# Seven quarter products in the last two stages of an attention, GLU and bilinear kernel

## The chip, the cores and the metric

One Trainium2 chip, one of its cores. The metric is the device time of one execution of the whole program in microseconds; a kernel's time is the median of its runs.

## What is computed

The reference is attention with a threshold (four batches, eight heads, 576 positions, head size 64), a gated layer, and a bilinear layer followed by two more matrix products. The change is in the last line of this cut:

```python
x = attn_out.transpose(0, 2, 1, 3).reshape(2304, 512)      # after the attention
g = x @ w_gate                                             # 512 x 1536, float64 on arrival
x = (g * sigmoid(g)) * (x @ w_val) @ w_out                 # 1536 x 512
h = (x @ w1) * (x @ w2)                                    # 512 x 1024 each
out = (h @ w3) @ w_out2                                    # 1024 x 1024, then 1024 x 512
```

[...]

## The kernel before

**Stages.** The program runs through attention; the first unit stage (the GLU, 12 units of 128 of the 1536 columns); the output stage (times `w_out`); the second unit stage (the bilinear product, 8 units of 128 of the 1024 columns); a stage that multiplies `w3` by `w_out2` once, so that the last stage, all 18 tiles of 128 tokens, is a single product with that 1024 x 512 matrix. Below, W is that product of weights, the stage that makes it is the W stage, and the stage after it is the last stage.

**Precision.** Every float32 operand is kept as two parts, a rounded one (`fp32r`) made by a cast on ScalarE and the rest made by a subtraction on VectorE (`rest_of`, L1594 to L1601, whose subtraction is recorded under L1589). A product is three passes (L1547, `mm3`): high by high, high by rest, rest by high. The passes of one accumulating group are matmuls of 128 x 128 weights with 512 or 256 columns.

**Units.** In both unit stages the tokens are four blocks of 512 and one of 256 (`blocks`, L1532). Two pairs of 512-blocks go through `seven` (L1756): their 1024 tokens and the two weight matrices form a 2 x 2 scheme that takes seven products in place of eight (p1 to p7, sums s1 to s4 of the inputs, differences of the weights); L1749 is its matmul, L1768 the copy that ScalarE takes of the running bank between two products, L1776 and L1780 VectorE's sums. The block of 256 goes through `plain` (L1827). Each unit also converts the weights of the next unit (`weights_f`, `weights_2`).

**Conversions to DRAM.** `whole_pair` (L1975) converts 128 x 1024 values of `w_out2` (4 calls) or `w3` (8 calls) and stores them in `v_dram`, from where the W stage loads them (`whole_back`, L2137 to L2141; the load is L2139). Its VectorE lines are L1631, L1634, L1639, L1643 and L1645, its ScalarE lines L426 and L427, its store L1659. Eight of the twelve calls are made in the first unit stage (L2024), three in the output stage (L2108, L2113), the last in the second (L2132).

**The last two stages.** Per group of 128 rows of W, `w3_turn` (L2150) loads a tile of `w3`, turns it with eight transposes (L2157) into two banks, and splits it (L2161, L2163); the group is then 24 matmuls of 512 columns (`go`, L2184), a cast and a subtraction (L2190, L2192). The last stage takes the blocks in the order 0, 1, 3, 4, 2; `h2_all` loads and splits a block (`h_two`: the load is L2034, with 2 KB in a row, the cast L2040), a tile is 24 matmuls of 512 columns, copied to SBUF by VectorE (L2225) or ScalarE (L2228) and stored (L2233).

**What orders the work.** `Program` (L125 to L296) takes steps with an engine, a cost, a due time and what they read and write, and lays all engines' instructions out before the run: an engine takes the step that can start first, by due time within 0.15 us; TensorE never takes one that is due more than 3 us after its oldest open step. Costs are written into the steps (0.6 us for a VectorE subtraction, 1.45 us for 12 matmuls of 256 columns, 4 us until a load has landed). The result is a fixed order for each engine's queue and for SyncE, which issues the transfers: an instruction whose input is late holds everything behind it. 42 tiles (`slot`, 128 x 2 x 512) are shared by all operands of these stages, four PSUM banks T and two double banks S by all products.

## Time and profile before

| | |
|---|---|
| median of three runs | 1071.97 us (1069.6 to 1074.06) |
| profiled execution | 1068.02 us, of which the span is 1066.2 |
| TensorE busy | 1042.2 us, 98% |
| VectorE busy | 838.8 us, 79% |
| ScalarE busy | 644.2 us, 60% |
| GpSimd busy | 286.4 us, 27% |
| DMA queue of SyncE | 161.29 MB, 50.1% of 16 engines |

How to read it: the span is what the engines' records cover; busy times are of that span. Shares over the whole span mix stages with different limits, so the rows further down are of single stages. A matmul's duration includes the way through the array, so the distance between starts says what one costs.

### The profile page before, as it was taken

To read this page: it belongs to the slowest core of one execution; us is meant where nothing else is said; L and a number is where in the kernel's file an instruction comes from. 1 tells how busy PE (TensorE), PEld (TensorE's weight loads), DVE (VectorE), ACT (ScalarE), POOL (GpSimd) and SP (SyncE) were. 2 spreads that over 40 slices of the span, in tenths; PEclk is the share of its full clock that TensorE was granted. 3 is DMA by queue.
4 is the path that set the end of the run, shared out by engine and by line. 5 is a ranking of instruction groups with operands and counts; after the bars stand their busy time and mean duration, and the time that the engine had idled before them with its cause. 6 is when DMAs were issued, how large, how long until landed. Compare 5 with 4: busy or idle time off the path is not lost.

```text
span 1066.2 us, 16931 instructions
## 1 busy us (share of the span) xinstructions
PE 1042.2 (98%) x5834; PEld 908.4 (85%) x5834; DVE 838.8 (79%) x1536; ACT 644.2 (60%) x1368; POOL 286.4 (27%) x307
## 2 busy tenths in 40 slices
PE   7999999999999999999999999999999999999998
PEld 6999999999977888888888889788888887888886
DVE  7999999999996979999999956976867777442320
ACT  6999999999974556656667634644433444242220
POOL 5899999999853000000000000000000000000000
PEclk9999999999999999999999999999999999999999
DMA  7686777766566225454556661551223225621531
GB/s 183 161 213 168 196 189 176 198 164 155 154 187 233 76 82 175 164 199 150 182 164 231 234 217 59 193 183 40 85 89 115 94 104 183 242 80 62 149 117 49
DMA packets 127206, 162.36 MB, mean 152 GB/s; under 512 B 48689, under 2 KB 83313, under 8 KB 127121
## 3 DMA queue, kind: packets, MB, share of 16 engines
q1 hardware_dynamic: 126976, 161.29, 50.1%
q8 instruction: 46, 0.75, 0.3%
q14 instruction: 40, 0.32, 0.1%
q10 hardware_dynamic: 144, 0.00, 0.0%
HBM read 93.47 MB, written 44.19 MB: 129 GB/s over the span
## 4 chain that ended last, share of the span: by engine, by line
PE 73%; DVE 12%; ACT 5%; DMA 4%; issue 2%; POOL 2%; SPq 1%; ACTq 0%; DVEq 0%; POOLq 0%
PE t_bank L1549 25%; PE t_bank L1749 16%; PE s_bank L1749 11%; PE s_bank L1549 6%; PE s_bank L627 5%; PE t_bank L591 4%; PE t_bank L869 3%; DVE slot L1589 2%; DVE P L675 2%; ACT P L684 1%; DVE E L659 1%; DMA x_dram<-xs 1%; POOL AT L376 1%; DMA slot<-v_dram 1%; PE t_bank L881 1%
## 5 line engine op out<-in xcount | busy, mean ns | idle before, releaser
L1549 PE MATMUL t_bank<-slot,slot 128*128 128x512 f32 (+1 forms) x1680 | 339.0, 360 | 1.4 <-DVE slot L1589 1.3
L1549 PEld LDWEIGHTS t_bank<-slot,slot 128*128 128x128 f32 x1680 | 283.9, 189 | 52.1 <-DVE slot L1589 2.4
L1749 PE MATMUL t_bank<-slot,slot 128*128 128x512 f32 x816 | 196.9, 390 | 1.2 <-ACT tmp L1768 1.2
L1589 DVE TENSOR_TENSOR slot<-slot,slot 128x512 fp32r<-128x512 f32 (+1 forms) x247 | 155.5, 664 | 41.7 <-ACT slot L2040 28.9
L1749 PEld LDWEIGHTS t_bank<-slot,slot 128*128 128x128 f32 x816 | 151.9, 188 | 32.8 <-ACT tmp L1768 2.1
L1749 PE MATMUL s_bank<-slot,slot 128*128 128x512 f32 x612 | 147.0, 389 | 0.0
L376 POOL TENSOR_TENSOR AT<-tmp,AT 128x512 fp32r<-128x512 f32 x105 | 137.5, 1309 | 8.8
L1749 PEld LDWEIGHTS s_bank<-slot,slot 128*128 128x128 f32 x612 | 114.9, 188 | 23.9
L1768 ACT COPY tmp<-t_bank 128x512 f32<-128x512 f32 x102 | 59.4, 584 | 114.0 <-PE t_bank L1749 113.9
L675 DVE SCALAR_TENSOR_TENSOR P<-s_bank,stat,E 128x576 f32<-128x576 f32 x144 | 116.4, 812 | 3.1
L684 ACT ACTIVATE P<-P,stat 128x576 f32<-128x576 f32 x144 | 112.6, 782 | 3.4 <-DVE P L675 1.2
L1597 ACT CAST slot<-slot 128x512 fp32r<-128x512 f32 x135 | 81.3, 621 | 53.4 <-DVE slot L1589 20.1
L659 DVE TENSOR_SCALAR_CACHE_REDUCE E<-s_bank,tau_sb 128x576 f32<-128x576 f32 x135 | 108.9, 810 | 4.7 <-PE s_bank L627 3.8
L627 PE MATMUL s_bank<-R,L 128*128 128x288 f32 x512 | 95.4, 308 | 7.9 <-DVE P L675 6.2
L627 PEld LDWEIGHTS s_bank<-R,L 128*128 128x128 f32 x512 | 74.1, 190 | 13.8 <-PE t_bank L591 2.7
L591 PE MATMUL t_bank<-ident,P 128*128 128x128 f32 x640 | 85.3, 273 | 0.4 <-DVE rt L1495 0.4
L1549 PE MATMUL s_bank<-slot,slot 128*128 128x512 f32 (+1 forms) x432 | 84.7, 354 | 0.0
L1549 PEld LDWEIGHTS s_bank<-slot,slot 128*128 128x128 f32 x432 | 71.5, 189 | 11.3
L426 ACT ACTIVATE raw<-raw,ebias 128x512 int32<-128x512 int32 x76 | 58.8, 774 | 29.4 <-DVE slot L1639 28.8
L2040 ACT CAST slot<-slot 128x512 fp32r<-128x512 f32 (+1 forms) x100 | 52.5, 577 | 38.5 <-DMA slot<-h_dram 34.0
L591 PEld LDWEIGHTS t_bank<-ident,P 128*128 128x128 f32 x640 | 73.9, 140 | 1.8 <-DVE rt L1495 0.7
L869 PE MATMUL t_bank<-AT,sp 128*128 128x288 f32 x448 | 74.1, 299 | 0.0
(156 smaller groups left out, 1342.8 us busy)
## 6 DMA issues: line engine op xcount, KB each, us to landing
slot<-h_dram SPq DMA_DIRECT2D x40, 512.0 KB
h_dram<-h SPq DMA_DIRECT2D x34, 512.0 KB
raw<-in_moe_w_dram SPq DMA_DIRECT2D x32, 512.0 KB
raw<-in_moe_w_out_dram SPq DMA_DIRECT2D x20, 512.0 KB
x_dram<-xs SPq DMA_DIRECT2D x64, 144.0 KB
L<-qlo SPq DMA_DIRECT2D x60, 128.0 KB
L<-qhi SPq DMA_DIRECT2D x60, 128.0 KB
raw<-in_moe_w_gate_dram SPq DMA_DIRECT2D x12, 512.0 KB
```

The costliest lines, as they stand in the source:

```text
L376: nc.gpsimd.tensor_tensor(out=lo, in0=src, in1=f32(hi), op=ALU.subtract)
L591: nc.tensor.matmul(bank[:, t * P:(t + 1) * P], lhsT=part, rhs=ident, is_transpose=True, start=(t == 0), stop=(t == len(parts) - 1),)
L627: nc.tensor.matmul(o, lhsT=lhs, rhs=R[:, c:c + HALF], start=(h == hs2[0] and e == 0), stop=(h == hs2[-1] and e == 1),)
L659: nc.vector.tensor_scalar(out=halves(t), in0=sb[:, :, 0:HALF], scalar1=tau_sb, scalar2=None, op0=ALU.add, op1=ALU.min, accum_out=st[:, 0, c],)
L675: nc.vector.scalar_tensor_tensor(out=halves(p_tile(p, i)), in0=sb[:, :, 0:HALF], scalar=st[:, 0, c], in1=halves(t), op0=ALU.is_gt, op1=ALU ...
L684: nc.scalar.activation(out=u, in_=u, func=ACTF.Exp, scale=-FAR, bias=st[:, 1, c], accum_out=sums[p // HP][:, c],)
L869: nc.tensor.matmul(b["t"][:, 0:HALF], lhsT=splits[p, 2][:, 4 * h + c, :, :].rearrange("p a d -> p (a d)"), rhs=AT[h][:, e, c, cs], start=( ...
L1549: nc.tensor.matmul(o, lhsT=lhs(a), rhs=rhs(c), start=(first and i == 0), stop=(last and i == 2))
L1589: nc.vector.tensor_tensor(out=out, in0=x, in1=y, op=ALU.subtract)
L1597: act(lambda: nc.scalar.copy(out=un["t"][:, 0, :], in_=src()), [key], [(un, 0)], 0.52, due, after)
L1749: nc.tensor.matmul(ap(), lhsT=un["t"][:, a, (off + kk) * P:(off + kk + 1) * P], rhs=x[kk]["ap"](c), start=(start and kk == 0 and i == 0), ...
L1768: act(lambda: nc.scalar.copy(out=k[n]["t"], in_=xa()), [(x, 0)], [(k[n], 0)], 0.47, NOW)
```

## The change

`quarters`, `rows_seven` and `stagger` bring a 2 x 2 scheme of seven products to the W stage and the last stage. Two 128-row tiles, each seen as two halves along the 1024 summed values, are the left side, the two halves of rows and of columns of the right matrix the right side; a product is 12 matmuls with 256 columns. The left side's sums s1 to s4 are made per pair of tiles (`quarters`: 11 VectorE operations and 7 casts), the right side's t1 to t4 once (`sums`: 8 subtractions and 8 splits). In `rows_seven` four products run one after the other in the same T bank, with a ScalarE copy after each, and three in two halves of an S bank, each ended by a VectorE addition. `stagger` puts p4 and p3 of one pair behind p1 of the next. W is kept as float32 too (`F["w"]`). The block of 256 tokens keeps the old form (`odd_tile`) and runs first. Loads of the left side in the last stage take 128 columns of all eight rows of `h2_dram` (`tile_in`), 512 bytes in a row. The calls of `whole_pair` in the output stage go to the second unit stage, one in each of the units 2 to 5, and the loads of `w_out2` may start one unit earlier.

The diff, cut to its core:

```diff
@@ rest_of: a list of keys may be given
+        keys = key if isinstance(key, list) else [key]
...
@@ output stage
     panels(0, True, (), 6.0, 1.2)
-    whole_pair(after=at_now(), due=12.0)
     weights_2(0, after=at_now(), due=16.0, step=2.0)
     for j in (2, 3, 4):
-        if j == 3:
-            for i in range(2):
-                whole_pair(after=at_now(), due=8.0 + 12 * i, step=1.6)
         banks = out_banks(j, j != 3)
...
@@ second unit
-        first = at_now()
+        before, first = first, at_now()
         if 1 <= f < NF2 - 1:
             weights_2(f + 1, after=first, due=4.0, step=1.6)
-        if f >= NF2 - 2:
-            whole_pair(after=first, due=4.0)
+        if f > 1:
+            whole_pair(after=first, due=8.0, step=1.6)
...
-    order = (0, 1, 3, 4, 2)
...
-        pe(5.46, go, [q for u in w3s + ps_ for q in both(u)], [(bank, 0)])
...
+    F, U_OF, SUMS = {"p": [], "w": []}, {"p": {}, "w": {}}, {}
     for c in range(NF2 // 2):
-        t = whole_back(c, -14.0 + 2 * c, first)
+        t = whole_back(c, -14.0 + 2 * c, before)
+        F["p"].append((t, both(t)))
+        for e in range(2 if c > 1 else 0):
+            U_OF["p"][2 * c + e] = rest_of(
+                lambda t=t, e=e: t["t"][:, e, :], (t, e), None, -14.0 + 2 * c)
...
+    def tile_in(c, due, after):
+        t = buf("slot", F32)
+        j = max(i for i in range(NB) if blocks[i][0] <= c)
+        sp(lambda: nc.sync.dma_start(
+            out=t["t"].rearrange("p e (f c) -> p (e f) c", c=P),
+            in_=h2_dram[:, :, c:c + P].rearrange("f p c -> p f c"),
+        ), [("h2", f, j) for f in range(NF2)], both(t), 1.2, 5.0, due - 6, after)
+        return t
...
+    def quarters(t, u, due, step=1.3):
+
+        A = {}
+        for key, b, e in (("11", t, 0), ("12", t, 1), ("22", u, 1)):
+            A[key] = half_of(b, e, due)
+            due += step
+        for key, op, o, x, y in (
+            ("s1", ALU.add, (u, 1), (u, 0), (u, 1)), ("s3", ALU.subtract, (u, 0), (t, 0), (u, 0)),
+            ("s2", ALU.subtract, (t, 0), (u, 1), (t, 0)), ("s4", ALU.subtract, (t, 1), (t, 1), (t, 0)),
+        ):
+            ap = lambda k: k[0]["t"][:, k[1], :]
+            dve(lambda o=o, x=x, y=y, op=op: nc.vector.tensor_tensor(
+                out=ap(o), in0=ap(x), in1=ap(y), op=op), [x, y], [o], 0.6, due)
+            A[key] = half_of(*o, due + 0.6)
+            due += step
+        return A
...
+    def sum_of(w, key, h, o, x, y, due):
+        at = lambda k: F[w][h + 2 * k[0]][0]["t"][:, :, k[1] * 256:(k[1] + 1) * 256]
+        on = lambda k: F[w][h + 2 * k[0]][1]
+        dve(lambda: sub(at(o), at(x), at(y)), on(x) + on(y), on(o), 0.6, due)
+        split_of(w, key, h, o, due)
+
+    def sums(w, due):
+        for key, *args in (
+            ("t1", (0, 0), (0, 1), (0, 0)), ("t3", (0, 1), (1, 1), (0, 1)),
+            ("t2", (1, 1), (1, 1), (0, 0)), ("t4", (1, 0), (1, 0), (1, 1)),
+        ):
+            for h in range(2):
+                sum_of(w, key, h, *args, due)
...
+        def product(bank, ap, un, key, start, stop):
+            ws = [right_of(w, key, kk) for kk in range(4)]
+
+            def go():
+                for kk in range(4):
+                    for i, (a, e) in enumerate(PASSES):
+                        nc.tensor.matmul(
+                            ap(), lhsT=un["t"][:, a, kk * P:(kk + 1) * P], rhs=ws[kk][1](e),
+                            start=(start and kk == 0 and i == 0), stop=(kk == 3 and i == 2),
+                            skip_group_check=not start,
+                        )
+
+            return pe(1.45, go, both(un) + [q for u, _ in ws for q in both(u)], [bank])
...
+        def p1():
+            product((x, 0), xa, A["11"], "11", True, False)
+            copy(top, 0)
+
+        def p2():
+            product((yz, 0), y, A["12"], "21", True, True)
+            plus(top, 0, y, (yz, 0))
+
+        def p6():
+            product((x, 0), xa, A["s2"], "t2", False, False)
+            copy(top, 1)
+
+        def p5():
+            product((yz, 1), z, A["s1"], "t1", True, False)
+
+        def p7():
+            product((x, 0), xa, A["s3"], "t3", False, False)
+            copy(low, 1)
+
+        def c22():
+            plus(low, 1, z, (yz, 1))
+
+        def p4():
+            product((x, 0), xa, A["22"], "t4", False, True)
+            copy(low, 0)
+            done(1)
+
+        def p3():
+            product((yz, 1), z, A["s4"], "22", False, True)
+            plus(top, 1, z, (yz, 1))
+            done(0)
+
+        return [p1, p2, p6, p5, p7, p4, p3, c22]
+
+    def stagger(chains, more, mid=lambda n, k: None):
+
+        old = None
+        for n, make in enumerate(chains):
+            more(n)
+            new = make()
+            if n + 1 == len(chains):
+                for chain, k in ((new, 0), (old, 5), (new, 2), (old, 6), (new, 4), (new, 3),
+                                 (new, 7), (new, 5), (new, 1), (new, 6)):
+                    chain[k]()
+                return
+            new[0]()
+            if old:
+                for go in old[5:7]:
+                    go()
+            for k, go in enumerate(new[1:5]):
+                go()
+                mid(n, k)
+            new[7]()
+            old = new
...
+    for n in range(2):
+        tiles = [last(2 * n + i, -14.0 + 3 * i + 6 * n, first) for i in range(2)]
+        QP.append(quarters(*[w3_turn(t) for t in tiles], -6.0 + 9 * n))
+        if n == 0:
+            for h in range(2):
+                split_of("p", "11", h, (0, 0), -12.0)
+            sums("p", -4.0)
...
+    def next_rows(n):
+        tiles = [tile_in(cols[n] + i * P, i, at_now()) for i in range(2)]
+        QS.append(quarters(*tiles, 0.0))
...
+        def done(e):
+            U_OF["w"][2 * n + e] = rest_of(outs[e]["ap"], keys[e], None, NOW)
...
+    def more_p(n):
+        if n < 2:
+            LOADED[:] = [last(2 * n + 4 + i, 0.0, at_now(4.0)) for i in range(2)]
+        if n >= 2:
+            ODDS.append(tile_whole(blocks[ODD][0] + (n - 2) * P, 2.0, at_now()))
+        if n == 3:
+            next_rows(0)
+
+    def mid_p(n, k):
+        if n < 2 and k < 2:
+            LOADED[k] = w3_turn(LOADED[k], k == 1)
+        if n < 2 and k == 2:
+            QP.append(quarters(*LOADED, 0.0))
+
+    stagger([lambda n=n: pair_of(n) for n in range(4)], more_p, mid_p)
...
+    for t in range(2):
+        part, end = odd_tile(t)
+        for fs in (range(4), range(4, 6), range(6, 7), range(7, 8)):
+            part(fs)
+        end()
+    sums("w", NOW)
+
+    def last_pair(n):
+        two = [buf("tmp") for _ in range(2)]
+        outs = [{"ap": lambda b=b: b["t"], "keys": both(b)} for b in two]
+        return rows_seven(
+            QS[n], "w", *outs, lambda e: store(two[e], cols[n] + e * P, both(two[e])))
+
+    stagger([lambda n=n: last_pair(n) for n in range(8)],
+            lambda n: n < 7 and next_rows(n + 1))
```

In the part that is left out, `w3_turn` turns two halves into one float32 tile (two T banks, or one S bank when `on_s` is set) with a plain ScalarE copy of each, and `half_of` and `split_of` are `rest_of` of one half.

## Rows read from the trace of the kernel before

**Rows 1.** The page: span, and busy time of each engine.

```profile
span 1066.2 us, 16931 instructions
PE 1042.2 (98%) x5834; PEld 908.4 (85%) x5834; DVE 838.8 (79%) x1536; ACT 644.2 (60%) x1368; POOL 286.4 (27%) x307
```

**Rows 2.** Windows: length; PE, PEld, DVE, ACT, POOL busy (instructions); clock; DMA share; GB/s.

```profile
466.00:488.00 22.00, 22.00 (x110) 18.70 (x109) 21.29 (x40) 13.88 (x23) 0.00 (x0) 1.00 0.53 176
...
794.00:816.00 22.00, 22.00 (x111) 18.70 (x110) 16.61 (x30) 8.87 (x15) 0.00 (x0) 1.00 0.29 102
...
882.00:904.00 22.00, 20.78 (x98) 16.82 (x97) 14.83 (x27) 9.13 (x17) 0.00 (x0) 1.00 0.64 221
...
970.00:1062.00 92.00, 92.00 (x407) 76.19 (x406) 21.76 (x37) 19.46 (x38) 0.00 (x0) 1.00 0.37 106
```

**Rows 3.** Timeline of the last stage: start, us, engine, line, operation, count.

```profile
969.79 92.64 PE L1549 MATMUL t_bank<-slot,slot 128*128 128x512 f32 x408
...
1062.47 0.69 DVE L2225 COPY tmp<-t_bank 128x512 f32<-128x512 f32 x1 [10.19 <-PE t_bank L1549]
```

**Rows 4.** Timeline of TensorE, output stage: the block of 256 tokens and what follows.

```profile
650.87 17.44 PE L1549 MATMUL s_bank<-slot,slot 128*128 128x256 f32 x144
668.15 14.02 PE L1549 MATMUL t_bank<-slot,slot 128*128 128x512 f32 x61
```

**Rows 5.** Timeline of TensorE in the W stage: two groups and their transposes.

```profile
927.25 1.04 PE L2157 MATMUL t_bank<-ident,slot 128*128 128x128 f32 x8
928.04 5.70 PE L1549 MATMUL t_bank<-slot,slot 128*128 128x512 f32 x24
933.59 1.03 PE L2157 MATMUL t_bank<-ident,slot 128*128 128x128 f32 x8
```

**Rows 6.** Timelines: where TensorE waits; in brackets idle time and releaser.

```profile
682.77 8.50 PE L1549 MATMUL t_bank<-slot,slot 128*128 128x512 f32 x36 [0.61 <-DVE slot L1589]
...
691.99 8.24 PE L1549 MATMUL t_bank<-slot,slot 128*128 128x512 f32 x35 [0.72 <-DVE slot L1589]
...
899.27 0.62 ACT L1597 CAST slot<-slot 128x512 fp32r<-128x512 f32 x1 [5.72 <-DMA slot<-v_dram]
...
900.43 1.66 PE L1749 MATMUL t_bank<-slot,slot 128*128 128x512 f32 x6 [0.38 <-ACT tmp L1768]
...
902.93 1.66 PE L1749 MATMUL t_bank<-slot,slot 128*128 128x512 f32 x6 [0.84 <-ACT tmp L1768]
...
915.03 1.25 PE L2157 MATMUL t_bank<-ident,slot 128*128 128x128 f32 x8 [0.36 <-DVE slot L1589]
```

**Rows 7.** Timeline: VectorE and ScalarE instructions back to back, and with 256 columns.

```profile
906.05 0.37 ACT L1852 COPY tmp<-t_bank 128x256 f32<-128x256 f32 x1 [0.64 <-PE t_bank L1549]
...
907.54 0.42 DVE L1859 TENSOR_TENSOR tmp<-tmp,t_bank 128x256 f32<-128x256 f32 x1 [1.02 <-issue]
...
970.48 2.71 ACT L2040 CAST slot<-slot 128x512 fp32r<-128x512 f32 x5
...
971.13 3.10 DVE L1589 TENSOR_TENSOR slot<-slot,slot 128x512 fp32r<-128x512 f32 x5 [3.46 <-ACT slot L2040]
```

**Rows 8.** Loads of 512 KB: issue (SPq), first cast, a slow landing.

```profile
981.91 0.94 SPq L2034 DMA_DIRECT2D slot<-h_dram  x2
...
986.71 1.83 ACT L2040 CAST slot<-slot 128x512 fp32r<-128x512 f32 x3 [5.24 <-DMA slot<-h_dram]
...
892.67 9.07 DMA slot<-v_dram
```

**Rows 9.** Packets of 970:1062 and 6:16; window 6:16; a 1024-packet issue.

```profile
DMA packets 5877, 9.77 MB, mean 106 GB/s; under 512 B 624, under 2 KB 1648, under 8 KB 5872
...
DMA packets 6192, 2.29 MB, mean 229 GB/s; under 512 B 5479, under 2 KB 5991, under 8 KB 6192
...
6.00:16.00 10.00, 6.54 (x53) 5.61 (x51) 6.87 (x14) 7.12 (x18) 7.13 (x10) 1.00 0.93 229
...
L574 SPq DMA_DIRECT2D ld<-in_k_dram x15: 607/659/679, 7.5 to 239.9; - x15
```

More of the change, by code (lines that the diff above doesn't have):

```diff
@@ L2156, in turn, with w3_turn @@
+    def w3_turn(t, on_s=False):
+        turned = buf("slot", F32)
+        two = [(buf("S"), 0)] if on_s else [(buf("T"), 0) for _ in range(2)]
+        for e in range(2):
+            b, _ = two[e % len(two)]
+            ap = lambda b=b, e=e: b["t"][:, e, :] if on_s else b["t"]
+            k = (b, e if on_s else 0)
+            def turn(e=e, ap=ap):
                 for c in range(4):
                     nc.tensor.transpose(
-                        b["t"][:, c * P:(c + 1) * P], t["t"][:, e, c * P:(c + 1) * P], ident)
@@ L2173 @@
[L2173 to L2194 removed]
+                        ap()[:, c * P:(c + 1) * P], t["t"][:, e, c * P:(c + 1) * P], ident)
@@ new lines, in half_of, with tile_whole @@
+    def half_of(t, e, due, after=()):
+        return rest_of(lambda: t["t"][:, e, :], (t, e), None, due, after)
+    def tile_whole(c, due, after):
+        t = tile_in(c, due, after)
+        return [half_of(t, e, due + e) for e in range(2)]
+    def quarters(t, u, due, step=1.3):
[13 more added lines that the diff above has]
+        return A
@@ new lines, in odd_tile, with part, go, end @@
+    def odd_tile(t):
+        bank, a = buf("T"), buf("tmp")
+        def part(fs):
+            def go():
+                for f in fs:
+                    mm3(bank["t"], lambda e: ODDS[t][f // 4]["t"][:, e, f % 4 * P:(f % 4 + 1) * P],
+                        lambda c: U_OF["w"][f]["t"][:, c, :], f == 0, f == NF2 - 1)
+            pe(0.682 * len(fs), go, [q for f in fs for u in (ODDS[t][f // 4], U_OF["w"][f])
+                                     for q in both(u)], [(bank, 0)])
+        def end():
+            dve(lambda: nc.vector.tensor_copy(out=a["t"], in_=bank["t"]), [(bank, 0)], [(a, 0)],
+                0.6)
+            store(a, blocks[ODD][0] + t * P, [(a, 0)])
+        return part, end
@@ new lines @@
+    last = lambda i, due, after: whole_back(NF2 // 2 + i, due, after)
+    QP = []
+    for n in range(2):
[5 more added lines that the diff above has]
+            sums("p", -4.0)
+    ODDS, QS, LOADED = [], [], []
+    cols = [c0 + t for c0, n in blocks if n == 512 for t in (0, 2 * P)]
```

106 lines of the change are left out of this document (44 added, 62 removed).

## The prediction

> **What bounds the kernel now.** I read the page first: TensorE is busy for 1042.2 of 1066.2 us [rows 1]. A busy TensorE need not be the limit, so the windows come next: in the unit stages and the last stage it has no idle time at all at full clock (22.00 of 22, 92.00 of 92), with VectorE at 97% in the first unit, 75% in the second and 24% in the last stage [rows 2]. The timelines then give the pace: the last stage is one unbroken row of 408 matmuls in 92.64 us, so 0.227 us each [rows 3], and nothing but TensorE's own work sets its length. The waits are few: two of 0.61 and 0.72 us in the output stage behind VectorE, and three of 0.38, 0.84 and 0.36 us where the second unit stage hands over to the W stage [rows 6]. What shortens TensorE's row in these stages shortens the kernel, as long as VectorE, ScalarE and the loads keep up.
>
> **TensorE's work.** The old form of two row tiles is 48 matmuls of 512 columns: 48 x 0.2267 = 10.88 us. The new one is 7 products of 12 matmuls with 256 columns. What such a matmul costs with new weights each time is in the trace: the output stage runs 144 of them from 650.87 to 668.15, so 0.1200 us each [rows 4], and a pair costs 84 x 0.1200 = 10.08 us. That is 0.80 saved, not an eighth, since half the columns cost more than half. There are 4 pairs in the W stage and 8 in the last: 12 x 0.80 = **9.6 us off**. The Trainium skill (TensorE: Matmul & The Clock Gate, Back-to-back issue gap) gives columns / 2.4 GHz + 2.5 ns from start to start, by which, as an estimate, a pair would go from 10.36 to 9.17 us and the sum be 14.2 us off; the trace is slower at both widths and decides. The 64 transposes of w3 stay (a group of 6.34 us holds 24 x 0.227 of matmuls, so 0.90 for eight of them [rows 5]); the block of 256 tokens stays as it is.
>
> **The conversions that move.** A call is ten VectorE and four ScalarE instructions, two loads and a store on SyncE. Away from the output stage they free VectorE where its subtractions came late twice: 0.61 + 0.72 = **1.3 us off**, between 0 (if other work of VectorE fills the place) and 1.3. In the second unit they meet units of the same matmuls as the first unit's, and the first unit does exactly this already: weights of the next unit and one such call, VectorE 21.29 of 22 us, DMA share 0.53, TensorE 22.00 [rows 2]. So they cost nothing there; their cover is VectorE's 5.4 us of idle time per window (16.61 of 22), and without it a call's 4.7 us (21.29 - 16.61) would show. On SyncE the two loads and the store stand among loads and stores as in the first unit.
>
> **The last stage.** In a pair's 10.08 us VectorE has 11 operations at 0.60 (five in 3.10 us, the last 0.69 long [rows 3, 7]) and 3 additions of 256 columns at 0.42: 7.9 us. ScalarE has 7 casts at 0.52 and 4 copies at 0.37: 5.1 us. Both fit. The copy between p6 and p7, in the same bank, has one product (1.44 us) to finish in; 0.37 and the hand-offs fit, if ScalarE is free. The end: an addition of 256 columns (0.42) in place of a copy of 512 (0.69 [rows 3]): **0.3 us off**.
>
> **The hand-over.** Here is the unknown. Before and within the W stage VectorE gets 44 operations for four `quarters`, 22 for the splits and sums of w_out2, 8 rests of W, 4 for the block of 256 tokens, 11 for the first pair of the last stage, 16 sums of W and 2 copies: 107 x 0.60, and 12 additions x 0.42, 69.2 us. Room: the last unit (84 x 0.2267 + 24 x 0.120 = 21.9 us, less 6.4 of its own), the W stage (4 x 10.08 + 8 x 0.90 = 47.5) and the tiles of the block of 256 (10.9): 73.9 us. That is 94% full, with chains in it: p6 of the first pair needs four transposed halves, copies, a cast, a subtraction, three sums, a cast and a subtraction, some 8 us, against 3.6 of transposes and 2.9 of p1 and p2. TensorE's wait lies between 0 (p5 and the next transposes fill in) and 8 us: the 33 operations before p7, 19.8 us all begun late, less the 12 us of transposes and products in front of it. The first unit runs at 97% of VectorE without a wait, the nearest row, so I take a value nearer to the lower end, **3.0 us on**. The three old waits, **1.6 us**, go: two came from a cast that stood 5.72 us on ScalarE for a load of w_out2, with a copy that TensorE needed behind it [rows 6], and these loads may now start a unit earlier.
>
> **The sum:** -9.6 - 1.3 - 0.3 + 3.0 - 1.6 = -9.8 us. The profiled execution takes 1068.0, so 1058.2 for one like it. It is 4 us below the median of the three runs, 1071.97; against the median the time is **1062 us**. A measurement here tells about 0.5% (5.4 us) from no change.
>
> **Rival 1: the hand-over starves TensorE.** The work before W is made late, because the 42 tiles are still held by the second unit's inputs (28) or VectorE comes late, and TensorE waits 5 to 8 us at the start of the W stage instead of 3. For it: 94% and the long chain. Against it: panels go free with each product of the last unit, and the loads can start early. Time: 1064 to 1067, around the border between faster and the same.
>
> **Rival 2, slower: ScalarE waits in line for a load in the last stage.** This is the mechanism of the 0.84 us wait [rows 6]: a cast waits for its load, and the copy after p6 stands behind it. A pair's loads are issued when the pair before starts; the copy is needed 7.4 us after that, and the cast of the second tile is put in front of it, since the plan counts on its landing after 6.2 us. With a landing at L us after the first issue p7 starts L + 0.6 + 0.5 later instead of at 8.6: the wait is L - 7.5 in each of 7 pairs. Now the first of two loads lands 4.8 us after its issue (981.91 to 986.71 [rows 8]). A tile is now 1024 pieces of 512 bytes instead of 256 of 2 KB. Pieces of 1.66 KB take 0.37 x 16 x 92 us / 5877 = 93 ns of an engine, pieces of 370 bytes 24 ns [rows 2, 9]; by the line between them 512 bytes take 31 ns, a tile 2.0 us in place of 1.5, and issuing it 0.66 in place of 0.47. That puts L near 7.5: just no wait. Against it stands the 9.07 us of a load that queued behind others [rows 8]. At L = 8.9 the gain is gone, at 9.07 the time is 1073, and from L = 9.7 (15 us in all) the kernel is slower by over 0.5%, at some 1078.
>
> **Rival 3: VectorE becomes the bound at the hand-over for its pace.** If an operation held the next one back for its whole 0.69 us, the 107 would need 9.6 us more, 78.8 in 73.9 us of room: 5 us of waits more, 1067. The Trainium skill states such a rule (VectorE: DVE Perf Modes, The DRAIN you can't avoid: the next operation starts when the pipeline is empty). Against it the row shows five starts 0.60 apart while each lasts 0.69 [rows 3, 7].
>
> **How the numbers follow.** Forecast 0.62 (1059 to 1065, all faster); rival 1 0.18, half of it beyond 1066.6, the border of the same; rival 2 0.12, from a loss of some us (half of it the same) to slower (0.06) and a little beyond for both together; rival 3 0.08, mostly the same, 0.02 slower where it joins rival 2. So faster 0.71, same 0.21, slower 0.08. The range: the low end is the sum without new waits (-12.8, 1059) less the spread of the runs, 1057.5; the high end takes in rival 1, rival 3 and most of the same side of rival 2, 1071.
>
> **What would show it.** In the changed kernel's profile: pairs in the last stage 10.1 us apart and TensorE without a gap there; the last stage some 91.5 us from the first matmul on the block of 256 tokens (16 x 0.227 x 3 + 80.6), in place of 98; windows of the second unit's third to sixth unit with VectorE near 21.3 and TensorE at 22.00 of 22; no wait behind L1589 in the output stage; DMA share in the last stage near 0.5. Rival 1 shows as gaps of TensorE behind a cast or subtraction of the left side in the first pair; rival 2 as ScalarE idle "until DMA" in each pair, followed by a gap of TensorE behind the copy; rival 3 as VectorE starts 0.69 apart. The prediction is wrong if 256-column matmuls go slower than 0.120 when banks change every 12, or if the gaps add up to more than 8 us.

## The result and the profile after

The changed kernel takes **1058.9 us** (median of 4 runs, 1058.07 to 1060.16); the kernel before, run beside it, 1070.8 (4 runs, 1067.61 to 1074.06). The ratio is 0.990, 95% interval 0.987 to 0.992. The forecast was 1062 us, between 1057.5 and 1071, and faster. The profiled execution is 1059.05 us, its span 1057.3.

In the changed kernel's line numbers L2244 is the matmul of `rows_seven`, L2256 its ScalarE copy, L2261 its VectorE addition, L2159 and L2163 the transposes and their copies, L1598 and L1589 the cast and subtraction of `rest_of`, L2195 the sums of `quarters`; L1750 and L1769 are the second unit's matmul and copy (L1749 and L1768 before).

The page's span and busy times, to be read against [rows 1]:

```profile
span 1057.3 us, 18049 instructions
PE 1034.1 (98%) x6266; PEld 924.1 (87%) x6266; DVE 918.8 (87%) x1675; ACT 693.4 (66%) x1469; POOL 285.8 (27%) x307
```

TensorE has 432 matmuls more and 8.1 us of busy time less; VectorE has 80.0 us more to do, and the share of the whole span says nothing of whether that hurts. So to the windows, with the columns of [rows 2]. The first two answer to the second unit's and the hand-over's there (the second is 6 us longer here), the third is the W stage, the last the eight pairs:

```profile
794.00:816.00 22.00, 22.00 (x111) 18.70 (x110) 20.97 (x40) 11.93 (x20) 0.00 (x0) 1.00 0.51 174
882.00:910.00 28.00, 28.00 (x141) 23.82 (x140) 23.43 (x41) 11.71 (x22) 0.00 (x0) 1.00 0.44 155
910.00:960.00 50.00, 48.78 (x404) 47.70 (x403) 45.36 (x77) 38.68 (x78) 0.00 (x0) 1.00 0.31 98
971.00:1052.00 81.00, 80.68 (x670) 80.28 (x669) 60.36 (x104) 39.03 (x82) 0.00 (x0) 1.00 0.50 140
```

The second unit now looks as the first did (VectorE 20.97 of 22, forecast 21.3; TensorE 22.00). The end of the second unit, 20.78 of 22 before, is full. In the last stage VectorE rose from 24% to 75%, and TensorE is still full but for 0.32 us. The W stage has VectorE at 91% and TensorE idle for 1.2 of 50 us. The list of TensorE's waits from the output stage on (us in total, times, longest) names what is left:

```profile
PE t_bank L2244 <- ACT slot L2256: 0.5, 1, 0.5
PE t_bank L2159 <- ACT slot L2163: 0.5, 1, 0.5
PE t_bank L2244 <- ACT tmp L2256: 0.3, 1, 0.3
PE t_bank L2244 <- DVE slot L1589: 0.2, 1, 0.2
```

Both waits of the output stage and all three of the hand-over [rows 6] are gone; four others are new, three of them in the W stage and one (0.3 us) in the last. TensorE's timeline, in the order of time:

```profile
669.57 32.83 PE L1549 MATMUL t_bank<-slot,slot 128*128 128x512 f32 x144
...
913.96 1.14 PE L2159 MATMUL t_bank<-ident,slot 128*128 128x128 f32 x8 [0.48 <-ACT slot L2163]
...
948.29 3.13 PE L2244 MATMUL t_bank<-slot,slot 128*128 128x256 f32 x24 [0.49 <-ACT slot L2256]
...
959.89 11.07 PE L1549 MATMUL t_bank<-slot,slot 128*128 128x512 f32 x48
...
991.43 1.70 PE L2244 MATMUL t_bank<-slot,slot 128*128 128x256 f32 x12 [0.32 <-ACT tmp L2256]
...
1001.61 3.04 PE L2244 MATMUL s_bank<-slot,slot 128*128 128x256 f32 x24
...
1011.69 3.04 PE L2244 MATMUL s_bank<-slot,slot 128*128 128x256 f32 x24
...
1021.77 3.04 PE L2244 MATMUL s_bank<-slot,slot 128*128 128x256 f32 x24
...
1049.37 3.04 PE L2244 MATMUL s_bank<-slot,slot 128*128 128x256 f32 x24
```

The first row is the stretch of the output stage that had the waits: 144 matmuls, 0.227 us each, unbroken. From 1001.61 on the same place of three pairs in a row is 10.08 us apart, twice: the forecast's price to the second decimal. The end of the program, on VectorE:

```profile
1052.45 0.76 DVE L2261 TENSOR_TENSOR tmp<-s_bank,tmp 128x256 f32<-128x256 f32 x2 [3.83 <-PE s_bank L2244]
```

Two additions, not one, stand behind the last product.

**The ledger.** Read from TensorE's first and last matmul of each stage (us; "output" from the end of the first unit's last matmul of seven products to the start of the second unit's first; "second" on to the first transpose of w3; "W and last" to TensorE's end; "tail" to the end of the span, which the page gives to 0.1 us):

| kernel | output | second | W and last | tail | sum | against before |
|---|---|---|---|---|---|---|
| before | 149.68 | 177.33 | 149.67 | 3.77 | 480.45 | |
| before, run again | 149.55 | 177.47 | 149.68 | 3.76 | 480.46 | +0.01 |
| changed | 147.70 | 175.53 | 142.00 | 4.89 | 470.12 | -10.33 |

"W and last" divides at the first matmul of the last stage (964.35 before, 959.89 after): W went from 51.59 to 49.48, the last stage from 98.08 to 92.52.

### The profile page after: what moved, and what is told of

Read it like the earlier page. It is cut to its first block, busy times and chain, and to the rows that moved or that the text cites. A ratio compares the mean times of both kernels' runs of the same rounds, so it can differ in the third digit from the quotient of the medians.

```text
span 1057.3 us, 18049 instructions
## 1 busy us (share of the span) xinstructions
PE 1034.1 (98%) x6266; PEld 924.1 (87%) x6266; DVE 918.8 (87%) x1675; ACT 693.4 (66%) x1469; POOL 285.8 (27%) x307
## 4 chain that ended last, share of the span: by engine, by line
PE 76%; DVE 10%; ACT 6%; DMA 3%; issue 2%; SPq 2%; POOL 0%; DVEq 0%; ACTq 0%; POOLq 0%
PE t_bank L1750 18%; PE t_bank L1549 16%; PE s_bank L1750 13%; PE s_bank L1549 8%; PE t_bank L2244 6%; PE s_bank L2244 5%; PE s_bank L627 3%; PE t_bank L591 3%; DVE P L675 3%; PE t_bank L869 2%; DVE E L659 2%; ACT P L684 2%; DVE slot L1589 1%; ACT tmp L801 1%; DMA ld<-in_k_dram 1%
## 5 line engine op out<-in xcount | busy, mean ns | idle before, releaser
L1589 DVE TENSOR_TENSOR slot<-slot,slot 128x512 fp32r<-128x512 f32 (+2 forms) x325 | 209.1, 678 | 37.9 <-ACT slot L2041 23.7
L1549 PE MATMUL t_bank<-slot,slot 128*128 128x512 f32 (+1 forms) x1104 | 206.4, 344 | 0.1
L1549 PEld LDWEIGHTS t_bank<-slot,slot 128*128 128x128 f32 x1104 | 176.3, 189 | 27.7 <-issue 1.7
L1750 PE MATMUL t_bank<-slot,slot 128*128 128x512 f32 x816 | 196.5, 390 | 0.0
L1598 ACT CAST slot<-slot 128x512 fp32r<-128x512 f32 x227 | 136.5, 622 | 76.0 <-DVE slot L2195 22.3
L1750 PEld LDWEIGHTS t_bank<-slot,slot 128*128 128x128 f32 x816 | 152.1, 188 | 30.9
L1750 PE MATMUL s_bank<-slot,slot 128*128 128x512 f32 x612 | 147.0, 389 | 0.0
L1750 PEld LDWEIGHTS s_bank<-slot,slot 128*128 128x128 f32 x612 | 114.9, 188 | 23.9
L1769 ACT COPY tmp<-t_bank 128x512 f32<-128x512 f32 x102 | 59.4, 582 | 105.4 <-PE t_bank L1750 105.4
L2244 PE MATMUL t_bank<-slot,slot 128*128 128x256 f32 x576 | 74.3, 284 | 1.0 <-ACT slot L2256 0.5
```

What stands on the lines that cost most here:

```text
L1549: nc.tensor.matmul(o, lhsT=lhs(a), rhs=rhs(c), start=(first and i == 0), stop=(last and i == 2))
L1589: nc.vector.tensor_tensor(out=out, in0=x, in1=y, op=ALU.subtract)
L1598: act(lambda: nc.scalar.copy(out=un["t"][:, 0, :], in_=src()), keys, [(un, 0)], 0.52, due, after)
L1750: nc.tensor.matmul(ap(), lhsT=un["t"][:, a, (off + kk) * P:(off + kk + 1) * P], rhs=x[kk]["ap"](c), start=(start and kk == 0 and i == 0), ...
L2244: nc.tensor.matmul(ap(), lhsT=un["t"][:, a, kk * P:(kk + 1) * P], rhs=ws[kk][1](e), start=(start and kk == 0 and i == 0), stop=(kk == 3 an ...
```

## The experiments

### The kernel before, again

No edit. The runs of before scatter over 6 us, half the gain, so the first question is where.

> The kernel before, unchanged, for a second profile and more runs. Its four runs reach from 1067.6 to 1074.1 us, those of the changed kernel only from 1058.1 to 1060.2, and the profile of before is one of its short runs. Theory S1: the spread sits in waits that the change took away (the load of w_out2 at the hand-over, 1.7 us of TensorE's starts in the profile shown): a longer run shows several us more between the start of the last second-unit unit and the last stage, and the rest alike within 0.5 us. Theory S2: the spread sits ahead of the change, at the end of attention, where the two profiles already differ by 1.4 us: then the first matmul of the first unit stage moves with the run's time, and what follows takes the same 758 us.

Measured: 1068.8 us median against 1070.0 for the same kernel's other runs, ratio 0.9992 (0.9978 to 1.0006). The profiled executions differ by 3.8 us of span, and the sums of the ledger's four stages by 0.01: theory S2. Their whole difference lies ahead, in the attention and the start of the GLU. One piece of it (1.1 us), a wait of TensorE at the start of the GLU, before and again:

```profile
336.98 0.73 PE L1931 MATMUL s_bank<-h,pick 8*128 8x512 f32 x2 [1.14 <-ACT slot L1948]
```

```profile
339.64 0.73 PE L1931 MATMUL s_bank<-h,pick 8*128 8x512 f32 x2 [2.23 <-ACT slot L1948]
```

Another 1.1 us follows right behind this row: from 341 to 344.4 us TensorE's granted clock is 0.50 (1.2 GHz) in the second execution, after it had stood still for 2.23 us, and in the first it stays at 1.00 (2.4 GHz) behind the wait of 1.14; from this row to the first product of seven they take 52.28 and 51.15 us. The other 1.6 us lie ahead of the row.

So single executions can be compared by the ledger to some 0.1 us, while medians need many runs for 1 us. All the runs below are read this way first.

### The moves alone, the products alone, the W stage alone

Moves: the kernel before, with

```diff
-    whole_pair(after=at_now(), due=12.0)           # output stage
...
-            for i in range(2):
-                whole_pair(after=at_now(), due=8.0 + 12 * i, step=1.6)
...
-        if f >= NF2 - 2:
-            whole_pair(after=first, due=4.0)
+        if f > 1:
+            whole_pair(after=first, due=8.0, step=1.6)
...
-        t = whole_back(c, -14.0 + 2 * c, first)
+        t = whole_back(c, -14.0 + 2 * c, before)
```

> Only the moves: no whole_pair in the output stage, one in each of units 2 to 5 of the second unit stage, loads of w_out2 a unit earlier; the W stage and the last stage in the old form. Theory that the terms add up: the output stage 2.0 us shorter (147.9 from its first matmul to the second unit), the second unit 175.5 in place of 177.3, so 3.7 us off the profiled 1068.0 and the median near 1067; windows of the second unit with VectorE near 21 of 22 and TensorE 22.00. Rival: the moves alone give nothing, since the waits at the hand-over come back behind another load or VectorE: 1070 to 1071. If S1 holds for the spread, its runs lie within 2 us of each other.

Products: the changed kernel, with the four `whole_pair` calls at their old places.

```diff
+    whole_pair(after=at_now(), due=12.0)           # output stage
...
-        if f > 1:
-            whole_pair(after=first, due=8.0, step=1.6)
+        if f >= NF2 - 2:
+            whole_pair(after=first, due=4.0)
```

> Only the seven products in the last two stages; the three whole_pair calls stay in the output stage and the last one in the second unit. Theory that the terms add up: W stage 49.5 us in place of 51.7, the eight pairs and the block of 256 92.4 in place of 98.0, the end 1.1 longer, the output stage with its two waits: 6.7 us off, plus up to 1.8 if the early loads alone cure the hand-over; median 1062 to 1064. Rival: the products need the moves, because VectorE has to have the hand-over's work prepared: then the W stage takes over 55 us and the median is above 1066.

W stage: the changed kernel, whose last stage takes all blocks by `h2_all` and 24 matmuls of 512 columns as before.

```diff
-    stagger([lambda n=n: last_pair(n) for n in range(8)],
-            lambda n: n < 7 and next_rows(n + 1))
+    for at, j in enumerate(order):
+        c0, n = blocks[j]
...
```

> The changed kernel with the last stage in its old form (18 tiles of 24 matmuls of 512 columns, loads with 2 KB in a row, blocks in the order 0, 1, 3, 4, 2). Theory that the terms add up: output stage -2.0, second unit -1.8, W stage -2.2 against before, last stage 98.0 again and the old end: 6 us off the profiled 1068.0, the median 1064 to 1065, so that the last stage in seven products is worth 5.6 less 1.1 of a longer end. Rival: the W stage in seven products gives nothing by itself (its waits eat the 3.2 us) and the last stage gives all: 1066 to 1067.

| kernel | median us (runs) | ratio, interval | output | second | W and last | tail | against before |
|---|---|---|---|---|---|---|---|
| moves | 1064.4 (7) | 0.9955, 0.9939 to 0.9971 | 147.70 | 175.52 | 149.67 | 3.79 | -3.77 |
| products | 1060.9 (6) | 0.9918, 0.9899 to 0.9937 | 149.54 | 175.52 | 142.03 | 4.85 | -8.51 |
| W stage | 1064.3 (6) | 0.9948, 0.9927 to 0.9968 | 147.69 | 175.53 | 146.87 | 3.75 | -6.61 |

In the ledger the three come out as their theories have it, within 0.6 us (3.7, 6.7 plus up to 1.8, and 6 us off). The medians agree with the ledger to 2 us only: that of "moves" is 2.6 us below the 1067 expected, that of "products" 1.1 below the lower end. The parts are nearly independent of each other. Taking the conversions out of the output stage is worth 1.98 us there, whatever the last stages do. The second unit's 1.8 us come with the early loads, which all three kernels have, and not with the conversions: they are in "products" too. And 3.77 + 8.51, less the 1.81 that both hold, is 10.47 against 10.33. The third wait of the hand-over (0.36, at a transpose) stays in "moves", whose "W and last" is that of before; it goes only with the new form of the W stage. The one interaction is in the W stage: 48.76 us in the third kernel, 49.48 in the changed one. It is the wait before 948.29, which the third kernel does not have: in the changed one the copy that TensorE needs runs at 947.87, behind two casts, of which the first had stood 2.83 us for a sum of VectorE (L2195), made 2.3 us later than in the third kernel. The changed kernel makes the first pair's sums for the last stage there too; that they make this sum late was not tried apart.

### The loads of w_out2 a unit later

```diff
-        t = whole_back(c, -14.0 + 2 * c, before)
+        t = whole_back(c, -14.0 + 2 * c, first)
```

> The changed kernel with the loads of w_out2 for the W stage started at the last unit again, as before, not one unit earlier. The run with the products alone lost both waits at the hand-over without the moved conversions, so the theory is that the early loads did that: here the second unit takes 177 us again (175.5 with early loads) and, since 22 VectorE operations hang on these loads, the W stage starts later too: 2 to 5 us in all. Rival: the early loads are worth nothing, because the panels of the last unit hold the tiles anyway: within 0.5 us of the changed kernel from the first product of the first unit stage to the end (667.7 us).

Measured: 1064.2 us (one run); the second unit 179.65, 4.12 us longer, the other stages within 0.3. ScalarE's timeline and then TensorE's, of this kernel:

```profile
902.73 0.62 ACT L1598 CAST slot<-slot 128x512 fp32r<-128x512 f32 x1 [2.31 <-DMA slot<-v_dram]
903.26 0.58 ACT L1769 COPY tmp<-t_bank 128x512 f32<-128x512 f32 x1
...
903.89 2.06 PE L1750 MATMUL t_bank<-slot,slot 128*128 128x512 f32 x6 [2.27 <-ACT tmp L1769]
```

The three rows are one sentence: the cast waits for its load, the copy stands behind the cast, TensorE needs the copy. It is the old wait of [rows 6] (0.84), in one piece and larger; what makes it larger was not tried apart. From start to start it costs 2.49 us (six matmuls from 900.04 on, so the next was due at 901.40). The other 1.63 lie behind it, in the row that follows, of this kernel and of the changed one:

```profile
905.74 4.19 PE L1549 MATMUL t_bank<-slot,slot 128*128 128x256 f32 x24
```

```profile
902.06 3.04 PE L1549 MATMUL t_bank<-slot,slot 128*128 128x256 f32 x24
```

From 905 to 908.3 us TensorE's granted clock is 0.50 (1.2 GHz), ahead of the wait and from 908.4 on 1.00 (2.4 GHz): matmuls of 256 columns start 0.213 us apart there in place of 0.120. It is the only stretch of lower clock within the ledger's four stages, up to TensorE's last product, of all these kernels. The edit `before` instead of `first` carries the second unit's gain, and without it the change would keep only 5.9 of its 10.3 us.

### Ten subtractions more on VectorE ahead of the W stage

```diff
-        dve(lambda: sub(part(1), at(), f32(part(0))), on + [(un, 0)], [(un, 1)], 0.6, due)
+        def rest():
+            for _ in range(2 if w == "p" else 1):
+                sub(part(1), at(), f32(part(0)))
+
+        dve(rest, on + [(un, 0)], [(un, 1)], 0.6, due)
```

> The changed kernel with each subtraction of the ten splits of w_out2 and its sums done twice (ten more VectorE operations, 6.0 us, in the last second-unit units and at the start of the W stage; the order is unchanged). Theory that VectorE is nearly the limit there (68.8 us busy in the 78 us from 882 to 960): half or more of the 6 us shows, the W stage at 53 us or more against 49.5. Rival: the hand-over's waits are those of a chain through ScalarE and VectorE, VectorE has its gaps where the ten are made, and less than 1 us shows.

Measured: 1058.4 us (one run). 6.0 us more work on VectorE cost 0.79 in the second unit and 0.03 behind it. The 0.79 is one wait of 0.5 (bracket) behind the copy L1769, which stood behind a cast that had waited 4.32 us for a subtraction of VectorE. All ten were made ahead of the W stage (the last ended 1.0 us before the first transpose, at 909.67), and not partly in it as expected. So the run shows that VectorE had room ahead of the W stage; whether it is the limit in the W stage, at 91%, it does not show. The rival's "less than 1 us" came.

### Two unread loads more per pair, then three

A load of 512 KB, issued ahead of the pair's own two, that nobody reads:

```diff
+    def unread(after):
+        r = buf("raw")
...
+        sp(lambda: nc.sync.dma_start(out=r["t"], in_=row_src(w3, 0)), [], both(r), 0.0, 5.0,
+           -8.0, after)
...
     def next_rows(n):
+        for k in range(2):                         # or 3
+            unread(at_now())
         tiles = [tile_in(cols[n] + i * P, i, at_now()) for i in range(2)]
```

> The changed kernel with two loads of 512 KB that nobody reads ahead of each pair's two loads in the last stage; the order on TensorE, VectorE and ScalarE is unchanged. Theory of the prediction's rival 2: the second tile lands about 3 us later (1.5 us each), past the point where its cast stands in front of the copy after p6, so TensorE waits 1 to 3 us in each of 7 pairs, 7 to 20 us in all, with ScalarE idle until the load. Rival: the plan leaves the loads several us of room, and the last stage stays within 1 us of 92.5.

Two of them: 1058.4 us (one run), and "W and last" 141.97, nothing at all. The same window of the changed kernel and then of this one:

```profile
971.00:1051.00 80.00, 79.68 (x662) 79.28 (x661) 60.36 (x104) 39.03 (x82) 0.00 (x0) 1.00 0.50 139
```

```profile
971.00:1051.00 80.00, 79.68 (x663) 79.31 (x662) 59.82 (x103) 39.51 (x82) 0.00 (x0) 1.00 0.77 219
```

The DMA share went from 0.50 to 0.77 and TensorE did not notice. Yet the casts did wait; a pair's issue and its casts, of this kernel:

```profile
996.26 1.05 SPq L2171 DMA_DIRECT2D slot<-h_dram  x2
...
1002.98 1.14 ACT L1598 CAST slot<-slot 128x512 fp32r<-128x512 f32 x2 [0.40 <-DMA slot<-h_dram]
1004.54 0.62 ACT L1598 CAST slot<-slot 128x512 fp32r<-128x512 f32 x1 [0.42 <-DMA slot<-h_dram]
```

The loads landed 6.7 and 8.3 us after their issue, in the pair two later 8.3 and 9.6 (issue 1015.69, casts 1023.97 and 1025.32). In the changed kernel the same casts wait for nothing; they are the last three of this row, whose first is the cast of a sum, so they start 7.6 us after the issue:

```profile
995.50 1.15 SPq L2171 DMA_DIRECT2D slot<-h_dram  x2
...
1002.61 2.18 ACT L1598 CAST slot<-slot 128x512 fp32r<-128x512 f32 x4 [0.43 <-DVE slot L2195]
```

So the reserve was there and its end had not been found. With a third load:

> The changed kernel with three more loads of 512 KB per pair of the last stage, issued ahead of the pair's own two and read by nobody, in place of two. With two of them the casts of the new tiles waited for the loads (landing 6.7 and 8.3 us after the pair's start) and TensorE did not wait. Theory (the slower rival of the prediction, with its threshold corrected): a third load puts the landings 1.4 to 1.6 us later again, near 8.2 and 9.8 us; the cast of the second tile then holds the copy behind p6, needed by about 9 us, and TensorE waits 0.5 to 1.5 us in each of 7 pairs, so the last stage is 3 to 10 us longer. Rival: the loads still come in time, since the plan puts these casts behind the copies that TensorE waits for: the last stage is within 0.3 us of 92.5 and no wait of TensorE stands behind ScalarE other than those of the changed kernel.

Measured: 1064.6 us (one run), "W and last" 146.26, 4.29 us more than with two; the other stages are unchanged. Its window, its list of TensorE's waits, and one pair on SyncE, ScalarE and TensorE:

```profile
971.00:1051.00 80.00, 76.94 (x622) 75.19 (x621) 61.82 (x105) 39.00 (x81) 0.00 (x0) 1.00 0.84 253
...
PE t_bank L2244 <- ACT tmp L2256: 2.9, 5, 0.8
...
1007.27 2.50 SPq L2353 DMA_DIRECT2D raw<-in_moe_w_dram  x3
1009.87 1.72 SPq L2171 DMA_DIRECT2D slot<-h_dram  x2
...
1018.72 1.14 ACT L1598 CAST slot<-slot 128x512 fp32r<-128x512 f32 x2 [3.09 <-DMA slot<-h_dram]
1020.24 0.62 ACT L1598 CAST slot<-slot 128x512 fp32r<-128x512 f32 x1 [0.37 <-DMA slot<-h_dram]
1020.76 0.36 ACT L2256 COPY tmp<-t_bank 128x256 f32<-128x256 f32 x1
...
1021.18 3.14 PE L2244 MATMUL t_bank<-slot,slot 128*128 128x256 f32 x24 [0.73 <-ACT tmp L2256]
```

This is rival 2 as it was written: load, cast of the second tile, copy, TensorE, in one line. Here the two loads land 8.9 and 10.4 us after their own issue (the three unread ones take 2.6 us of SyncE before it) and TensorE starts 0.9 us late; with the second tile at 9.6, with two unread loads, it lost nothing. The direct line is not most of the loss. In the three pairs from 1003.32 to 1037.57 us, 4.0 us longer together than 30.24, it cost 0.3, 0.9 and 0.1. The other 2.7 us come some 3.6 to 3.9 us later in the same pairs, at three further waits of the list:

```profile
1013.00 1.70 PE L2244 MATMUL t_bank<-slot,slot 128*128 128x256 f32 x12 [0.49 <-ACT tmp L2256]
...
1024.74 1.69 PE L2244 MATMUL t_bank<-slot,slot 128*128 128x256 f32 x12 [0.42 <-ACT tmp L2256]
...
1036.04 1.69 PE L2244 MATMUL t_bank<-slot,slot 128*128 128x256 f32 x12 [0.76 <-ACT tmp L2256]
```

There the copy stands behind casts of sums, and VectorE makes these sums (L2195) only behind the subtractions that the late casts feed: its first begins 0.4 us after TensorE's row of these matmuls (1009.82 against 1009.38), in the changed kernel 0.4 us ahead of it (1006.95 against 1007.37). The theory expected 3 to 10 us; 4.3 came, by two paths and not by one.

### Another order at the end

The pairs' columns rotated by one, so that the last pair's tiles are stored in one piece each, and another order of the last pair's products (n0 to n7 are its p1, p2, p6, p5, p7, p4, p3 and its other addition, o5 and o6 are p4 and p3 of the pair before):

```diff
+    cols = cols[1:] + cols[:1]
...
-                for chain, k in ((new, 0), (old, 5), (new, 2), (old, 6), (new, 4), (new, 3),
-                                 (new, 7), (new, 5), (new, 1), (new, 6)):
+    LAST_ORDER = ("n0", "o5", "n1", "o6", "n2", "n3", "n4", "n7", "n6", "n5")    # first try
+    LAST_ORDER = ("n0", "o5", "n2", "o6", "n4", "n3", "n7", "n1", "n5", "n6")    # second try
```

> The changed kernel with another order at its end: the pair of tokens 0 to 255, whose tiles are stored in one piece each, comes last, and in the last pair p2 comes third and p4 last, so that only a copy of 256 columns and one store stand behind the last matmul. Theory that the longer end (4.9 us from TensorE's last matmul to the end of the span, against 3.8 before) comes from two additions in a row and a tile stored in two pieces: the end is 3.6 to 3.8 us, 1.1 us off, the rest unchanged. Rival: the end is the landing of the stores, which queue behind six others: 4.5 us or more.

First try: 1058.4 us (one run). The tail is 3.79 in place of 4.89, but "W and last" grew by 0.75, for p4 follows p7 in the same bank with nothing between. The plan laid p3 behind p4 after all, so an addition ends this kernel too, and not a copy as expected:

```profile
1049.67 1.70 PE L2244 MATMUL t_bank<-slot,slot 128*128 128x256 f32 x12 [0.46 <-ACT tmp L2256]
```

> The changed kernel, with the last pair's products in the order p1, p4 and p3 of the pair before between them as now, then p6, p5, p7, its other addition, p2 ahead of p4 and p3, and p4 and p3 exchanged for the end so that one addition of 256 columns stands behind the last product, and with the columns of the pairs rotated by one, so that the last pair's tiles are stored in one piece each. In the run before it (order p4 right behind p7) the tail fell by 1.1 us and 0.75 us came back as a wait of TensorE, because p7's copy had nothing between it and p4 in the same bank. Here a product in the other bank stands between every two that share one. If that is the whole reason, the time from TensorE's last product to the span's end is 3.7 to 4.0 us (4.89 in the changed kernel) and the stretch from the first transpose of w3 to TensorE's end stays at 142.0 to 142.1 us, so the kernel is about 1.0 us (0.1%) faster than the changed one, at a median near 1058. Rival: the three copies of ScalarE that then follow each other at the end are late whichever the order; TensorE keeps a wait of 0.3 to 0.7 us in the last pair and the net is 0.4 us or less.

Second try: "W and last" 142.04, tail 3.82, so 1.03 us less than the changed kernel in the ledger and the best of all (11.36 less than before), as expected. The median of its 4 runs, 1059.6 us (1058.45 to 1059.84; ratio 0.9896, 0.9877 to 0.9914), does not show it; 1 us is less than the runs of one kernel differ by, and the profiled execution reached the first unit's seven products 1.8 us later than the changed kernel's did. The end of this kernel on VectorE:

```profile
1051.49 0.76 DVE L2261 TENSOR_TENSOR tmp<-s_bank,tmp 128x256 f32<-128x256 f32 x2 [3.95 <-PE s_bank L2244]
1054.31 0.42 DVE L2261 TENSOR_TENSOR tmp<-s_bank,tmp 128x256 f32<-128x256 f32 x1 [2.06 <-PE s_bank L2244]
```

One addition behind the last product, then 3.37 us to the span's end (1058.1 - 1054.73); in the changed kernel 4.09 (1057.3 - 1053.21). The second addition cost 0.34. The other 0.72 is the time from the last addition to the end, put down to the store in two pieces; the rotation was not run without the new order.

## Why the prediction was right, and where its terms were off

| term | forecast us | measured us |
|---|---|---|
| 12 pairs at 10.08 in place of 10.88 | -9.6 | -9.6 |
| new waits in the W stage | +3.0 | +2.0 |
| new waits in the last stage | 0 | +0.8 |
| output stage | -1.3 | -1.98 |
| old waits of the hand-over | -1.6 | -2.7 |
| tail | -0.3 | +1.1 |
| sum | -9.8 | -10.3 (ledger) |

The middle rows come out of the ledger with the forecast's own prices: a W stage without a wait would be 8 x (24 x 0.2267 + 0.90) = 50.7 before and 4 x 10.08 + 7.2 = 47.5 after, against 51.59 and 49.48; a last stage 10.88 + 8 x 10.08 = 91.5, and 0.16 for the last matmul's way, against 92.52. The old hand-over is 1.80 in the second unit and 0.86 in the W stage. The terms add up to -10.4, the ledger's sum within 0.1.

The main term is right by its mechanism. That the sum lies only 0.5 from the forecast is in part luck: the five others are off by 0.7 to 1.4 us each, to both sides, and nearly cancel.

**Products.** The step "half the columns cost more than half" held: 0.1200 us per matmul, also where the bank changes every 12. Of the two sums the forecast weighed, 9.6 and the 14.2 worked out from the Trainium skill (TensorE: Matmul & The Clock Gate, Back-to-back issue gap), the rows decide for 9.6: by the formula of the Trainium skill a pair is, as an estimate, 9.17 us, and the pairs measured are 10.08. That section of the Trainium skill gives this formula for a single matmul taken alone, and not for a stream with a weight load at each, which this is; the forecast left that out.

**Output stage.** Right in cause: the waits stay in "products" (two, 1.3 us, behind L1589) and go in "moves". Mis-sized: the forecast took 0.61 + 0.72 as what is to be had. TensorE's row ahead of the first of them, in the kernel before:

```profile
674.75 7.41 PE L1549 MATMUL t_bank<-slot,slot 128*128 128x512 f32 x32
```

32 x 0.2267 = 7.25, so the next matmul was due at 682.00 and started at 682.77: 0.77 lost, not 0.61, because idle time counts only from the end of the last matmul's way through the array, 0.16 later. The 36 matmuls behind the wait last 8.50 where 36 x 0.2267 + 0.16 is 8.32: 0.18 more. Each wait so costs 0.34 above its bracket, two of them 2.0 in place of 1.33. Nearly the same holds for the old hand-over: brackets of 0.38 and 0.84, and 1.80 us in the second unit.

**Hand-over.** Two errors, both to the safe side. The old waits were worth 2.7, not 1.6, for the reason above and since the W stage's start held more than the one bracket of 0.36. The new ones are 2.0 and not 3.0; the choice "nearer to the lower end", from the first unit's VectorE at 97% without a wait, was the right one. The subtractions added show that VectorE had room ahead of the W stage; that it has room within it no run shows. Two of the three waits there are behind copies of ScalarE; the longest of them goes back to VectorE, since a cast in front of that copy had stood 2.83 us for a sum. **Rival 1** did not come (2.0 us, not 5 to 8); late loads would have cost 4.1 us, but in the second unit, by ScalarE's queue (2.5) and by slower matmuls behind the wait, nearly all at the lower granted clock (1.6), not by tiles that were held.

**Last stage.** Called free of waits, it has one in the list: the copy before 991.43 stood behind two casts and another copy on ScalarE, and these behind a cast that had waited 1.83 us for a sum of VectorE. Two places together, 0.6 us there and 0.24 at 1027.53 to 1032.09 (36 matmuls in 4.56 us of starts, where 4.32 is the price), make the 0.8. "ScalarE is free" was not looked at copy by copy.

**Rival 2.** The mechanism is real and its place was right; its threshold and slope were wrong, and it is the smaller part of what the third unread load cost. The forecast put the cast of the second tile ahead of the copy behind p6 at 6.2 us, from the plan's cost of a landing. In the plan that was made the casts stand 7.6 us behind the issue, behind the copies due by then. So at a landing of 9.6 us, where the forecast's "L - 7.5" gives 2.1 us for the pair, nothing is lost; at 10.4, where it gives 2.9, the direct loss is 0.9. The changed kernel itself is far from either: none of its casts waits for a load in the last stage, with 512 bytes in a row.

**Rival 3.** Subtractions that do not touch each other's tiles stay 0.60 apart, and the ten added ones cost 0.8 us in all. Two rows of the changed kernel, three subtractions and two sums:

```profile
990.32 1.89 DVE L1589 TENSOR_TENSOR slot<-slot,slot 128x512 fp32r<-128x512 f32 x3
...
998.42 1.42 DVE L2195 TENSOR_TENSOR slot<-slot,slot 128x512 f32<-128x512 f32 x2
```

Three in 1.89 us are 0.60 apart. The two sums, where the second writes over what the first reads, are 0.73 apart: there the next one does wait out the whole 0.69, which the forecast's price of 0.60 for all eleven operations left out. The rule of the Trainium skill (VectorE: DVE Perf Modes, The DRAIN you can't avoid), by which an operation would hold back the next until the pipeline is empty, is not what the first row shows; the same section of the Trainium skill adds that an operation that is not held starts earlier, and the first row agrees.

**Tail.** The sign was wrong. The step "an addition of 256 columns in place of a copy of 512" counted one instruction; there are two additions behind the last product and a store in two pieces, 1.1 us more than before in place of 0.3 less. The first addition does not start with the end of its own product, 1.4 us before the other. Both products lie in the two halves of one S bank; the second try has the same where p5 and p2 follow each other in one S bank (both additions behind the second, at 1051.49). Where two products in a row lie in different S banks, as from 1001.61 on, the first addition starts with the end of its own:

```profile
1003.25 0.42 DVE L2261 TENSOR_TENSOR tmp<-s_bank,tmp 128x256 f32<-128x256 f32 x1 [0.67 <-PE s_bank L2244]
```

So it goes with the shared bank; why, no run here tells.

**The number.** 1068.02 - 10.33, and 1.4 us more that this execution spent ahead of the first unit's seven products, is 1059.1; measured 1059.05. The 1.4 us are one stretch of lower clock near the end of the attention, the same eight matmuls before and after:

```profile
304.43 1.32 PE L1365 MATMUL t_bank<-AT,sp 128*128 128x288 f32 x8 [0.71 <-ACT xs L1381]
```

```profile
304.40 2.29 PE L1365 MATMUL t_bank<-AT,sp 128*128 128x288 f32 x8 [0.71 <-ACT xs L1381]
```

From 304.4 to 307.7 us the granted clock is 1.00 (2.4 GHz) in the first and 0.50 (1.2 GHz) in the second. That the forecast against the median was 3 us too high comes, for 1.9 of them, from the median of three runs: 18 runs of before have theirs at 1070.0, not 1071.97. The rest is the 0.5 of the sum and the scatter of the medians.

## What to carry over

Price a narrower form of a product by rows of the same width in the same kernel; it gave the main term exactly where half the columns would have promised half the time. Count a wait from start to start, not by the idle column. For each instruction that ends late, ask what stands in front of it in its own engine's queue: four of this case's waits (the old hand-over, the late loads, the third unread load, the one at 991.43) are a short copy of ScalarE behind casts, although VectorE is the busier of the two throughout. Then ask what the casts wait for: a load in the first three, a sum of VectorE in the last and in most of what the third unread load cost. And compare the granted clock behind a long wait before putting all of a loss down to the wait.

## What was not expected

- DMA share rose from 0.50 to 0.77 for the same 0.32 us of TensorE's idle time; at 0.84 the loss was 4.3 us. What the rows tie the loss to is not the share but the landing against the order of one engine.
- Two executions of one kernel 3.8 us apart have the same 480 us from the output stage on, within 0.01 us in sum: their difference lies wholly ahead of it.
- Late loads cost 4.1 us, of which the wait itself is 2.5: behind it the granted clock was 0.50 for a stretch.
- Behind a wait the first matmuls of TensorE run 0.1 us (256 columns: 1.70 in place of 1.60 for 12) to 0.18 us (512 columns) longer than the same group without one.
